# The cast of the second batch's first piece goes from GpSimd to ScalarE, in four parts, and four steps of a hand-set schedule change their visits

## The chip, the cores and the metric

The kernel runs on one core of one Trainium2 chip. The metric is the device time of one execution, in microseconds (us), lower is better. Every time below is of that one core. TensorE is called PE, VectorE DVE, ScalarE ACT, GpSimd POOL, and SyncE, which only issues DMAs here, SP.

## The reference

Per batch, 32 inducing vectors attend to the 12480 rows of `x` (giving `h`), then every row of `x` attends to the 32 rows of `h`; the result goes through a two-layer block with a PReLU-like step.

```python
B, N, m, C = (4, 12480, 32, 128)
n_tokens, d_model, d_ff = (49920, 128, 2048)

def mab(q, kv):
    s = scale * (q @ kv.transpose(0, 2, 1))
    s = s - s.max(-1, keepdims=True)
    a = np.exp(s)
    a /= a.sum(-1, keepdims=True) + 1e-09
    return a @ kv
h = mab(I, x)
x = mab(x, h).reshape(B * N, C)
h = x @ w_in
g = np.maximum(h, 0.0) + alpha * np.minimum(h, 0.0)
out = g @ w_out
```

## The kernel before, in words

**Tiles.** A batch's 12480 rows are cut into "supers" `s` of 2048 rows (16 tiles of 128), and a short rest of 192 rows. The first attention of a batch works on *pieces*, which are these supers in the order 0, rest, 1, 2, 3, 4, 5. `whole_pieces[p]` has index `p`, so the second batch's first piece is p=0 (super 0), its second is the short rest, the third p=2 (super 1), the fourth p=3 (super 2).

**First attention, per piece.** `a_load` brings the rows in as f32 (`xs`, 1024 KB, four buffers), `a_cast` makes them bf16 (`xn`, one POOL instruction of 128x2048, line 330), `a_turn` turns them by a DMA transpose on SP's queue (`xT`, line 353), `a_scores` and `a_least` give scores and their extreme, `a_exp` the exponentials `e1T` (ACT), `a_e1` turns those by a DMA transpose on SP's queue (line 446), `a_h`/`a_add` sum up. `a_cast_part` is a variant of the cast for a part of a piece, on an engine of choice; the start of the program uses it for the first batch (lines 347 and 349).

**Second attention, per super ("second rows").** Eight steps: `b_scores` (PE, line 641, and a copy from PSUM by ACT or DVE), `b_max` (DVE, line 718), `b_less_pool` (POOL, line 723), `b_exp` (ACT, line 685), `b_sum` (POOL: five additions of line 709 and `den`, line 733), `b_rec` (DVE, `rc`, line 746), `b_mul` (POOL, writes the attention weights four times over, `rep`, line 754), `b_turn` (a DMA transpose on SP's queue, `a<-rep`, line 763). Its result `a2` is what the second stage below multiplies.

**Blocks and visits.** The main loop goes over *visits*. A block is four tiles (512 rows) of one super; it has four visits, and a super 16. In a visit PE makes four products `hh` of 32x512 (`visit`, line 805, needs `a2` of its super), ACT and DVE turn each into a `gt` by ReLU (lines 818 and 820), and then PE makes the 16 products of the visit before (`second`, line 831). The linear part (line 858) is added by pairs of blocks. A finished block is copied out of PSUM (`finish`, lines 877, 884, 886) and stored by a DMA on SP's queue (line 891). The first super of the first batch is scaled only there, by the reciprocal `rec3` (`first_rec`, line 1164), whose sums POOL makes in `first_sum` (lines 709, 1151).

**What sets the order.** All work other than the main loop's is hung on visits by number with `at(n, fn, ..., cost=...)` and is issued after visit n's products, in the order in which it was registered: first the second-rows steps of all supers, then the pieces by p. Engines run their instructions in that order. SP's queue is in order as well: a DMA whose data isn't ready holds those behind it. `Plan.choose` searches, from hand-given costs of each step, which ReLU goes to ACT ("a") and which to DVE ("v"), which PSUM bank each product takes, and whether a step issued through `plan.then` runs in its visit or waits ("l") until the third ReLU of the next visit. It doesn't count POOL, nor DMAs.

For the first batch's super s=1 the visits of the eight steps are written by hand (`when`), and it is needed from visit 16 on; super 2 of the first batch is needed from visit 32 on. For the second batch's pieces p=0 to 3 the visits of load, cast and turn are written by hand too; p=0 is loaded ahead of the main loop. Scores of p=0 are at visit 19, of p=2 at 22, of p=3 at 30.

```python
            when = [1, 2, 3, 4, 5, 8, 8, 9]
```

```python
                load, cast, turn = {
                    0: (-1, 4, 6), 1: (-1, 9, 10), 2: (4, 10, 12), 3: (7, 16, 17)
                }.get(p, (load, cast, turn))
```

Of the kernel before, what the change touches and what calls it, by code (L numbers as in the profile page):

```python
# [24 lines left out]
BT = 4  # L25
# [5 lines left out]
def kernel(  # L31
# [239 lines left out]
    plan = Plan()  # L271
# [14 lines left out]
    def new_state(b):  # L286
        st = State()
        st.b = b
        st.pieces = whole_pieces if b else first_pieces
        st.np = len(st.pieces)  # L290
        st.xT = xt_pool.tile([C, NT, P], bf16, name="xT", tag="xT")
        st.xn, st.xs, st.s1, st.e1T, st.e1, st.s1p, st.hp = {}, {}, {}, {}, {}, {}, {}
        st.e2, st.m2, st.den2, st.rc, st.rep = {}, {}, {}, {}, {}

        st.mx = sm_pool.tile([P, NX], f32, name="mx", tag="mx")
        st.rm = sm_pool.tile([P, NX], f32, name="rm", tag="rm")
        st.fac = sm_pool.tile([P, NX], f32, name="fac", tag="fac")
        st.da = sm_pool.tile([P, NX], f32, name="da", tag="da")
        st.ex = sm_pool.tile([P, NX], f32, name="ex", tag="ex")
        st.den = sm_pool.tile([P, 1], f32, name="den", tag="den")  # L300
        st.hs = h_pool.tile([P, C], f32, name="hs", tag="hs")
        eng = nc.gpsimd if b else nc.vector
        eng.memset(st.mx[:], HIGH)
        eng.memset(st.da[:], 0.0)
        return st
# [18 lines left out]
    def a_cast(st, pc):  # L324
        s = pc.s
        r0, nt, last = supers[s]
        xs = st.xs[s]
        if pc.full:
            st.xn[s] = xn_pool.tile([P, ST, C], bf16, name="xn", tag="xn")
            nc.gpsimd.tensor_copy(out=st.xn[s][:], in_=xs[:])  # L330
        else:
            st.xn[s] = xn_left
            for t in range(nt):
                n = last if t == nt - 1 else P
                nc.gpsimd.tensor_copy(out=xn_left[:n, t, :], in_=xs[:n, t, :])

    def a_cast_part(st, pc, t0, n, eng):
        s = pc.s
        if not pc.full:
            a_cast(st, pc)  # L340
            return
        if s not in st.xn:
            st.xn[s] = xn_pool.tile([P, ST, C], bf16, name="xn", tag="xn")
        ts = slice(pc.t0 + t0, pc.t0 + t0 + n)
        to, of = st.xn[s][:, ts], st.xs[s][:, ts]
        if eng == "a":
            nc.scalar.copy(out=to, in_=of)
        else:
            (nc.gpsimd if eng == "p" else nc.vector).tensor_copy(out=to, in_=of)

    def a_turn(st, pc):
        s, nt = pc.s, pc.n
        nc.sync.dma_start_transpose(
            out=st.xT[:, tile0[s] : tile0[s] + nt, :],
            in_=st.xn[s][:, :nt, :].rearrange("p j c -> p (j c)"),
        )
# [326 lines left out]
    def b_exp(e, n):  # L683
        def work():
            nc.scalar.activation(out=e[:, :n], in_=e[:, :n], func=EXP, scale=scale)  # L685

        plan.then(work)
# [219 lines left out]
    st = new_state(0)  # L907
# [127 lines left out]
    def begin(step):  # L1035
# [39 lines left out]
        if f in "tc":  # L1075
            t0, n = cuts[pc.n][int(part)]
            if f == "t":
                kept["t", p, part] = a_turn_pe(st, pc, t0, n)
            else:
                a_turn_copy(st, pc, t0, n, kept.pop(("t", p, part)), act)  # L1080
        elif f == "k":
            a_cast_part(st, pc, *cuts[pc.n][int(part)], step[-1])
            done = first_pieces[int(p)].s
            if pc.full and step == last_cast[done]:
                load_next(done)
            if step == weights_after:
                load_weights()
        elif f == "u":
            kept["u", p] = a_e1_pe(st, pc)
        elif f == "v":  # L1090
            a_e1_copy(st, pc, kept.pop(("u", p)), act)
        else:
            {"s": a_scores, "m": a_least, "e": a_exp, "f": a_fac, "h": a_h, "g": a_add}[f](st, pc)
# [100 lines left out]
    def at(n, fn, *args, cost=()):  # L1194


        todo.setdefault(max(n, 0), []).append((fn, args, cost))
# [15 lines left out]
    for b, s, nt in groups[1:]:  # L1213
        n = first[b, s]
        when = [n - 23, n - 19, n - 16, n - 14, n - 13, n - 11, n - 9, n - 6]
        if (b, s) == (0, 1):
            when = [1, 2, 3, 4, 5, 8, 8, 9]
        if (b, s) == (0, 2):
            when[7] = n - 7
        at(when[0], on, b, b_scores, s, nt, cost=[("s", 25 * nt), ("f", 0)])  # L1220
        at(when[1], on, b, b_max, s, nt, cost=[("v", 70 + 33 * nt)])
        at(when[2], on, b, b_less_pool, s, nt)
        at(
            when[3],
            lambda b=b, s=s, nt=nt: b_exp(states[b].e2[s], nt),
            cost=[("a", 100 + 27 * nt)],
        )
        at(when[4], on, b, b_sum, s, nt)
        at(when[5], on, b, b_rec, s, nt, cost=[("v", 160)])
        at(when[6], on, b, b_mul, s, nt)  # L1230
        at(when[7], on, b, b_turn, s, 0, nt)
# [6 lines left out]
    def small_at(n, fn, *args, cost):  # L1238


        (kind, ns), *rest = cost
        at(n, fn, *args, cost=[(kind, ns + (0 if n in shared else TURNED)), *rest])
        shared.add(n)

    for b in range(B - 1):
        n = first[b, 0] - 1
        if b:
            at(n - 4, lambda b=b: states.__setitem__(b + 1, new_state(b + 1)))
        for p, pc in enumerate(whole_pieces):
            m = n + (8 * (p - 1) if p > 1 else p)  # L1250
            load, cast, turn = m - 3, m + 6, m + 8
            score = m + 15 if p > 1 else n + 16
            look = score + 1 + (p == 1)
            join = m + (24 if p == whole_pieces[-1].k else 23) if p > 1 else n + (31 if p else 23)
            if not b:
                load, cast, turn = {
                    0: (-1, 4, 6), 1: (-1, 9, 10), 2: (4, 10, 12), 3: (7, 16, 17)
                }.get(p, (load, cast, turn))
                score, look = (score, look) if p > 1 else (score + 4, look + 4)
                join = n + 31 if p < 2 else n + 39 if p < 4 else join  # L1260
            f = pc.full
            if load >= 0:
                at(load, on, b + 1, a_load, pc)
            at(cast, on, b + 1, a_cast, pc)
            at(turn, on, b + 1, a_turn, pc)
            small_at(
                score,
                on,
                b + 1,
                a_scores_least,  # L1270
                pc,
                cost=[("s", 215 if f else 85), ("v", 800 if f else 460)],
            )
            at(look, on, b + 1, a_exp, pc, cost=[("a", 717 if f else 430)])
            at(look + 2, on, b + 1, a_fac, pc, cost=[("a", 220)] if p else [])
            at(look + 1, on, b + 1, a_e1, pc)
            small_at(
                join, on, b + 1, a_h_add, pc, cost=[("s", 226 if f else 115), ("v", 260)]
            )
        m = n + 8 * (NS - 2) + 15  # L1280
        at(m + 2, on, b + 1, a_max, cost=[("a", 200)])
        at(m + 4, on, b + 1, a_factors, cost=[("s", 400), ("v", 70), ("a", 205)])
        at(m + 6, on, b + 1, a_parts, cost=[("a", 220), ("v", 260)])
        at(m + 8, on, b + 1, a_den, cost=[("s", 200), ("v", 370)])
        at(m + 12, on, b + 1, a_sum, cost=[("s", 200), ("v", 110)])
        small_at(m + 14, on, b + 1, a_w_both, cost=[("s", 220), ("a", 487)])
        small_at(m + 14, on, b + 1, a_lin, cost=[("s", 75), ("v", 190)])
# [4 lines left out]
    for n, (blk, i) in enumerate(visits):  # L1292
# [9 lines left out]
        cost = nt * Plan.FREE if both else 0  # L1302
# [55 lines left out]
```

## Time and profile before

| | |
|---|---|
| three runs | 597.59, 598.14, 598.18 us; median 598.14 us |
| the profiled execution | 596.33 us |
| its span in the trace | 594.5 us (1.83 us lie around it) |
| PE busy | 585.3 us, 98% of the span |
| DVE, ACT busy | 533.6 us (90%), 537.1 us (90%) |
| POOL busy | 218.6 us (37%) |
| granted TensorE clock | 1.0 |

Times in the trace count from the span's start. The main loop's first products stand at 30.0 us; a visit without extra products of PE takes 1.33 us. The table below gives, for finding one's way in the trace, where the `hh` products of a visit start.

| visit | 4 | 5 | 6 | 7 | 8 | 9 | 10 | 12 | 15 | 16 |
|---|---|---|---|---|---|---|---|---|---|---|
| us | 35.85 | 37.18 | 38.51 | 40.73 | 42.22 | 44.02 | 46.59 | 49.36 | 53.55 | 54.88 |

A group of instructions on one line of a timeline starts at the first column, lasts as long as the second, and may have in brackets the idle time of its engine before it and what ended it.

### The profile page before, as it was taken

What the parts mean: (1) busy time and instruction counts of PE and PEld (TensorE: products, weight loads), DVE (VectorE), ACT (ScalarE), POOL (GpSimd) and SP (SyncE); (2) the same over time, 40 slices, a digit from 0 to 9 for tenths busy, and PEclk for the clock granted to TensorE, in tenths of its full rate; (3) what the DMA queues carried; (4) which work ended last, traced back from release to release, by engine and by line L of the source; (5) the groups of instructions that cost most, each with busy time, mean ns of one, the idle gap of its engine ahead of it and who ended that gap; (6) DMA issues with size and microseconds to landing.
All of it is one profiled execution on the core that took longest, in us unless ns stands there. A gap on an engine that the chain in (4) does not pass through costs nothing.

```text
span 594.5 us, 23142 instructions
## 1 busy us (share of the span) xinstructions
PE 585.3 (98%) x9500; PEld 441.6 (74%) x9500; DVE 533.6 (90%) x975; ACT 537.1 (90%) x1085; POOL 218.6 (37%) x261
## 2 busy tenths in 40 slices
PE   9998999999999999999999999999999999999997
PEld 6676777777777777777777777777777777777776
DVE  5877999998999899998999989999999999989996
ACT  5787999999899999999999999999999998989986
POOL 3496525313416436323236156134134134144010
PEclk9999999999999999999999999999999999999999
DMA  8959799233177999541367999831321341433421
GB/s 340 272 176 222 186 233 176 70 100 83 45 205 159 242 205 198 126 82 55 78 162 171 192 238 195 170 92 46 91 72 55 92 75 53 118 76 65 91 69 47
DMA packets 122347, 80.56 MB, mean 136 GB/s; under 512 B 103760, under 2 KB 106112, under 8 KB 119168
## 3 DMA queue, kind: packets, MB, share of 16 engines
q1 hardware_dynamic: 122016, 78.99, 56.1%
q8 instruction: 74, 1.21, 0.9%
q14 instruction: 33, 0.27, 0.2%
q10 hardware_dynamic: 224, 0.09, 0.1%
HBM read 28.07 MB, written 25.56 MB: 90 GB/s over the span
## 4 chain that ended last, share of the span: by engine, by line
PE 89%; DMA 1%; POOL 1%; issue 0%; DVE 0%; DVEq 0%; ACT 0%
PE bp L831 63%; PE hh L805 21%; PE bp L858 2%; PE hh L641 1%; DMA a<-rep 1%; PE hh L470 1%; PE hh L376 1%; POOL rep L754 1%; DVE gt L820 0%; DVEq L1353 0%; PE hh L595 0%; PE hh L518 0%; PE hh L579 0%; PE hh L564 0%; PE hh L515 0%
## 5 line engine op out<-in xcount | busy, mean ns | idle before, releaser
L818 ACT ACTIVATE gt<-hh 128x512 bf16<-128x512 f32 x857 | 456.2, 604 | 38.4 <-PE hh L805 33.2
L820 DVE TENSOR_SCALAR gt<-hh 128x512 bf16<-128x512 f32 x703 | 451.4, 683 | 26.2 <-PE hh L805 14.8
L831 PE MATMUL bp<-W,gt 128*128 128x128 bf16 x6240 | 417.4, 220 | 0.3 <-DVE gt L820 0.2
L831 PEld LDWEIGHTS <-gt 128*128 128x128 bf16 x6240 | 349.3, 98 | 85.4 <-issue 76.6
L805 PE MATMUL hh<-a,HW 32*128 32x512 bf16 (+2 forms) x1664 | 156.0, 370 | 2.1 <-DMA a<-rep 1.6
L754 POOL TENSOR_TENSOR rep<-e,rc 128x2048 bf16<-128x2048 f32 (+1 forms) x24 | 84.5, 3521 | 25.7 <-DVE rc L746 25.3
L723 POOL TENSOR_TENSOR e<-e,smx 128x512 f32<-128x512 f32 (+1 forms) x24 | 24.6, 1027 | 158.1 <-ACT gt L818 81.3
L805 PEld LDWEIGHTS <-HW 32*128 32x128 bf16 x1664 | 40.6, 91 | 43.2 <-issue 7.2
L709 POOL TENSOR_TENSOR t<-e 128x256 f32<-128x256 f32 (+1 forms) x24 | 17.2, 718 | 139.8 <-ACT e L685 139.8
L884 ACT COPY ob<-bp 128x512 f32<-128x512 f32 (+1 forms) x62 | 36.3, 585 | 4.3 <-PE bp L831 1.4
L330 POOL CAST xn<-xs 128x2048 bf16<-128x2048 f32 x18 | 34.0, 1891 | 0.5
L709 POOL TENSOR_TENSOR t<-t 128x128 f32<-128x128 f32 (+3 forms) x100 | 30.5, 305 | 7.8
L886 DVE COPY ob<-bp 128x512 f32<-128x512 f32 x32 | 21.9, 685 | 6.1 <-PE bp L831 6.1
L858 PEld LDWEIGHTS <-a 32*128 32x128 bf16 x392 | 15.0, 93 | 6.0 <-issue 0.3
L390 DVE TENSOR_SCALAR_CACHE_REDUCE s<-hh 128x512 f32<-128x512 f32 (+2 forms) x29 | 17.9, 618 | 1.6 <-PE hh L376 1.6
L858 PE MATMUL bp<-HA,a 32*128 32x128 bf16 x392 | 19.1, 214 | 0.0
L415 ACT ACTIVATE e1T<-s,rm 128x512 bf16<-128x512 f32 (+1 forms) x25 | 17.9, 718 | 0.7 <-DVE rm L399 0.7
L718 DVE TENSOR_REDUCE smx<-e 128x16 f32<-128x512 f32 (+1 forms) x24 | 15.9, 661 | 0.0
L960 PE MATMUL bp<-blank 128*128 128x256 bf16 x78 | 14.4, 322 | 1.2 <-DVE blank L906 1.2
L685 ACT ACTIVATE e<-e 128x512 f32<-128x512 f32 (+1 forms) x24 | 15.0, 624 | 0.0
L699 ACT COPY e<-hh 128x512 f32<-128x512 f32 (+1 forms) x23 | 13.9, 604 | 0.7 <-PE hh L641 0.6
L486 DVE SCALAR_TENSOR_TENSOR hs<-hs,fac,hh 128x128 f32<-128x128 f32 (+1 forms) x25 | 8.6, 344 | 6.5 <-PE hh L470 5.5
(110 smaller groups left out, 201.5 us busy)
## 6 DMA issues: line engine op xcount, KB each, us to landing
out_dram<-ob SPq DMA_DIRECT2D x97, 256.0 KB, 2.6
xs<-in_x_dram SPq DMA_DIRECT2D x23, 1024.0 KB, 6.3
xs<-in_x_dram SPq DMA_DIRECT2D x2, 512.0 KB, 9.0
w_in_f<-in_moe_w_in_dram SPq DMA_DIRECT2D x1, 1024.0 KB, 4.8
a<-rep SPq DMA_TRANSPOSE x25, 5.2
xT<-xn SPq DMA_TRANSPOSE x18, 5.4
e<-e1T SPq DMA_TRANSPOSE x18, 2.7
xs_left<-in_x_dram SPq DMA_DIRECT2D x4, 64.0 KB, 5.0
```

What stands on the lines that cost most here:

```text
L330: nc.gpsimd.tensor_copy(out=st.xn[s][:], in_=xs[:])
L390: nc.vector.tensor_scalar(out=s1[:parts, :cols], in0=ps[:parts, :cols], scalar1=-scale, scalar2=None, op0=MULT, op1=MIN, accum_out=st.mx[: ...
L709: nc.gpsimd.tensor_tensor(out=t[:, :n], in0=src[:, :n, :w], in1=src[:, :n, w : 2 * w], op=ADD)
L723: nc.gpsimd.tensor_tensor(out=st.e2[s][:, :n], in0=st.e2[s][:, :n], in1=st.m2[s][:, :n].unsqueeze(2).broadcast_to([P, n, M]), op=SUB,)
L754: nc.gpsimd.tensor_tensor(out=rep[:, :n], in0=st.e2[s][:, :n].unsqueeze(2).broadcast_to([P, n, R, M]), in1=rc[:, :n].unsqueeze(2).unsqueez ...
L805: nc.tensor.matmul(hh[:, q * cols + w.start : q * cols + w.stop], HWs[b][rows, v * P : (v + 1) * P], a2[rows, t0 : t0 + nt, :].rearrange(" ...
L818: nc.scalar.activation(out=gt[:, :cols], in_=hh[:, :cols], func=RELU)
L820: nc.vector.tensor_relu(gt[:, :cols], hh[:, :cols])
L831: nc.tensor.matmul(blk.acc[:, t * C : (t + 1) * C], gt[:, (q * nt + t) * P : (q * nt + t + 1) * P], W1[:, k, :], start=(not blk.begun), st ...
L858: nc.tensor.matmul(blk.acc[w, t * C : (t + 1) * C], blk.a2[rows, blk.t0 + t, w], HAs[b][rows, :], start=(not blk.begun and t == 0), stop=F ...
L884: nc.scalar.copy(out=ob[:, :nt], in_=acc)
L886: nc.vector.tensor_copy(out=ob[:, :nt], in_=acc)
```

## The change

- The cast of the second batch's p=0 leaves POOL (visit 4, one instruction of 128x2048). It becomes four ACT copies of 128x512, issued through `plan.then` in visits 4, 5, 5 and 6, each with a cost of 560 ns of ACT in the plan; its DMA transpose goes from visit 6 to 7.
- For the second rows of super 1 of the first batch, `b_rec` goes from visit 8 to 7 and `b_turn` from 9 to 8. `b_mul` stays at 8.
- p=2 is cast at visit 9 instead of 10 and turned at 11 instead of 12.
- p=3 is loaded at visit 12 instead of 7, cast at 20 instead of 16 and turned at 21 instead of 17.

```diff
+    def a_cast_act(st, pc, t0, n):
+        plan.then(lambda: a_cast_part(st, pc, t0, n, "a"))
...
         if (b, s) == (0, 1):
-            when = [1, 2, 3, 4, 5, 8, 8, 9]
+            when = [1, 2, 3, 4, 5, 7, 8, 8]
...
                 load, cast, turn = {
-                    0: (-1, 4, 6), 1: (-1, 9, 10), 2: (4, 10, 12), 3: (7, 16, 17)
+                    0: (-1, -1, 7), 1: (-1, 9, 10), 2: (4, 9, 11), 3: (12, 20, 21)
                 }.get(p, (load, cast, turn))
...
-            at(cast, on, b + 1, a_cast, pc)
+            if cast >= 0:
+                at(cast, on, b + 1, a_cast, pc)
+            else:
+                for q, v in enumerate((4, 5, 5, 6)):
+                    at(v, on, b + 1, a_cast_act, pc, q * BT, BT, cost=[("a", 560)])
```

## The prediction

> **What bounds the kernel now.** The page comes first, for the engine shares and the chain of work that ended last.
>
> ```profile
> PE 585.3 (98%) x9500; PEld 441.6 (74%) x9500; DVE 533.6 (90%) x975; ACT 537.1 (90%) x1085; POOL 218.6 (37%) x261
> ...
> PE 89%; DMA 1%; POOL 1%; issue 0%; DVE 0%; DVEq 0%; ACT 0%
> ```
>
> PE is busy for 98% of the span and carries 89% of the chain. The change removes no PE work, so it can win only what PE waits. Where it waits is in the table of waits, asked for the stretch of the edited visits, 37 to 57 us:
>
> ```profile
> DVE rc L746 <- POOL den L733: 1.8, 1, 1.8
> PE hh L805 <- DMA a<-rep: 1.6, 1, 1.6
> ...
> PE hh L641 <- DVE ob L877: 0.7, 1, 0.7
> ```
>
> PE waits twice here, and the timeline of PE places both waits:
>
> ```profile
> 42.69 0.40 PE L858 MATMUL bp<-HA,a 32*128 32x128 bf16 x8
> ...
> 46.11 0.55 PE L641 MATMUL hh<-hT,xT 128*128 128x32 bf16 x16 [0.70 <-DVE ob L877]
> ...
> 56.57 0.40 PE L805 MATMUL hh<-a,HW 32*128 32x512 bf16 x4 [1.62 <-DMA a<-rep]
> ```
>
> One is 0.70 us at visit 9, for the PSUM bank that DVE's first `ob` copy frees; the other 1.62 us at visit 16, for the turned second rows of super 1. Together 2.32 us, the most that this place can give. Their common cause stands in the timelines of POOL and DVE.
>
> ```profile
> 40.80 1.89 POOL L330 CAST xn<-xs 128x2048 bf16<-128x2048 f32 x1
> 42.66 0.73 POOL L709 TENSOR_TENSOR t<-e 128x256 f32<-128x256 f32 x1
> ...
> 45.02 0.20 POOL L733 TENSOR_SCALAR den<-t 128x16 f32<-128x16 f32 x1
> 45.65 3.61 POOL L754 TENSOR_TENSOR rep<-e,rc 128x2048 bf16<-128x2048 f32 x1 [0.42 <-issue]
> ```
>
> ```profile
> 42.34 0.29 DVE L618 CAST HA<-hh 128x128 bf16<-128x128 f32 x1 [0.40 <-PE hh L616]
> 42.75 0.69 DVE L820 TENSOR_SCALAR gt<-hh 128x512 bf16<-128x512 f32 x1
> 45.26 0.25 DVE L746 RECIPROCAL rc<-den 128x16 f32<-128x16 f32 x1 [1.82 <-POOL den L733]
> 45.43 1.22 DVE L877 TENSOR_TENSOR ob<-bp,rec 128x512 f32<-128x512 f32 x2
> ```
>
> POOL makes the cast of the second batch's p=0 ahead of the sums of the second rows. So `den` is late; DVE, in order, stands 1.82 us before the reciprocal with the `ob` copies behind it (first wait); and `rep` starts at 45.65, after which SP's queue and the landing of its transpose decide:
>
> ```profile
> 42.72 1.92 SPq L353 DMA_TRANSPOSE xT<-xn  x1
> 44.68 1.28 SPq L315 DMA_DIRECT2D xs<-in_x_dram  x1
> 46.09 0.94 SPq L891 DMA_DIRECT2D out_dram<-ob  x2
> 49.29 3.60 SPq L763 DMA_TRANSPOSE a<-rep  x1
> ```
>
> ```profile
> 49.29 7.24 DMA a<-rep
> ```
>
> The second row is from the chain in order of time: issue to landing took 7.24 us, up to 56.53.
>
> **The change part by part.** *The cast leaves POOL.* Its slot is 42.66 - 40.80 = 1.86 us. The sums take 45.22 - 42.66 = 2.56 us, so `den` is there at 40.80 + 2.56 = 43.36 instead of 45.22.
>
> *`b_rec` one visit earlier.* It now follows `HA` of visit 7, which ends at 42.63. DVE waits 43.36 - 42.63 = 0.73 us instead of 1.82; behind the waiting instruction are one ReLU of visit 8 (0.69 us) and the `ob` copies. Reciprocal 43.40 to 43.65, ReLU to 44.3, first `ob` copy (half of 1.22) to about 44.9; its block is closed on PE by 43.09. PE wants the bank at 46.11 - 0.70 = 45.41. The first wait goes, with 0.5 us to spare.
>
> *`rep` and its turn.* `rep` followed the start of the reciprocal by 45.65 - 45.26 = 0.39 us and the turn followed `rep`'s start by 3.64, so it is issued at 43.40 + 4.03 = 47.43 instead of 49.29. All turns of this kind landed as in this row of the view of the tile `a`, and the one next after, whose row in the DMA view follows, in 4.4 us:
>
> ```profile
> DMA to landing us min/median/max: 2.7/5.2/7.2
> ```
>
> ```profile
> a<-rep SPq DMA_TRANSPOSE x1, 4.4
> ```
>
> It lands at 50.1 to 54.6, by the median at 52.6. Visit 16 would want it at 56.57 - 1.62 - 0.70 = 54.25. I take the median, as the 1024 KB load that preceded it at 44.68 moves to visit 12, behind it: no wait, 1.6 us to spare. At 7.2 us, 0.4 us of wait stay. Issuing the turn in visit 8 instead of 9 costs nothing, as no DMA stands between.
>
> [...]
>
> *Four casts on ACT.* Their price is between back-to-back work on ACT (4.04 / 8 = 0.505 us) and the same cast at the program's start (0.62 us):
>
> ```profile
> 49.84 4.04 ACT L818 ACTIVATE gt<-hh 128x512 bf16<-128x512 f32 x8 [0.24 <-PE hh L805]
> ```
>
> ```profile
> L347 ACT CAST xn<-xs x5: 602/619/1058, 6.2 to 17.9; 128x512 bf16<-128x512 f32 x3, 128x1024 bf16<-128x1024 f32 x2
> ```
>
> So 2.0 to 2.5 us more for ACT in visits 4 to 7. What hides them is idle time of ACT and DVE, by stretches (columns: length, then PE, PEld, DVE, ACT, POOL busy):
>
> ```profile
> 37.00:41.25 4.25, 4.25 (x69) 3.26 (x67) 3.01 (x8) 3.67 (x9) 3.79 (x9) 1.00 0.59 123
> 41.25:46.10 4.85, 4.16 (x68) 3.16 (x66) 2.51 (x6) 4.60 (x9) 4.03 (x8) 1.00 1.00 219
> ```
>
> Idle in the first: ACT 4.25 - 3.67 = 0.58, DVE 4.25 - 3.01 = 1.24, together 1.82. In the second: 0.25 and 2.34, together 2.59, of which 1.82 was the blocked reciprocal. The plan knows the casts' price and can move ReLUs to DVE. What doesn't fit into the first stretch is 0.2 to 0.7 us, on two engines 0.1 to 0.35 us of delay; PSUM banks leave little slack, so I take 0.3 us of PE. Bounds: no gain, since work is only added; at worst all four fall on PE's path, 2.5 us.
>
> [...]
>
> ```profile
> L349 DVE CAST xn<-xs x2: 427/556/686, 6.2 to 6.5; 128x512 bf16<-128x512 f32 x1, 128x1024 bf16<-128x1024 f32 x1
> ```
>
> On DVE the four would be 4 x 0.427 = 1.7 us, which fits into the 1.82 idle; by it the sum would be 0.3 us better than what I give the change.
>
> *p=2 one visit earlier* costs nothing: its cast still comes after `rep` on POOL, its turn after the second rows' turn on SP.
>
> *p=3 later.* Its cast comes to POOL at visit 20, ahead of `rep` of super 2, which ran from 66.91 and ended at 70.52, while SP took it only at 73.16: 2.6 us of slack for a cast of 1.89.
>
> ```profile
> 66.91 3.61 POOL L754 TENSOR_TENSOR rep<-e,rc 128x2048 bf16<-128x2048 f32 x1 [1.62 <-DVE rc L746]
> ```
>
> Its turn goes into SP's queue at visit 21, behind the first row here and ahead of the others; the last is super 2's turn:
>
> ```profile
> 66.13 1.19 SPq L446 DMA_TRANSPOSE e<-e1T  x1
> 67.42 1.81 SPq L446 DMA_TRANSPOSE e<-e1T_left  x1
> 70.81 1.64 SPq L446 DMA_TRANSPOSE e<-e1T  x1
> 72.54 0.53 SPq L891 DMA_DIRECT2D out_dram<-ob  x1
> 73.16 2.42 SPq L763 DMA_TRANSPOSE a<-rep  x1
> ```
>
> ```profile
> L353 SPq DMA_TRANSPOSE xT<-xn x18: 1339/3227/6987, 42.7 to 376.9; - x18
> ```
>
> ```profile
> 80.20 0.61 PE L805 MATMUL hh<-a,HW 32*128 32x512 bf16 x4
> ```
>
> All in the old kernel's clock, since this stage moves forward as a whole: 67.32 + d + 1.81 + 1.64 + 0.53 = 71.30 + d is when super 2's turn is issued, d being the issue time of p=3's turn (1.3 to 7.0, median 3.2); with landing L it must be there by 80.20. No wait while d + L is under 8.9 us. Medians: 3.2 + 5.2 = 8.4. I take no wait.
>
> *The plan.* `choose` runs anew, and every ReLU after visit 4 may change engines. Bounds from what PE's weight loads wait for ReLUs from 57 us to the end:
>
> ```profile
> PEld L831 <- DVE gt L820: 1.3, 6, 0.4
> ...
> PEld L831 <- ACT gt L818: 0.5, 2, 0.2
> ```
>
> Between -1.8 (all gone) and +1.8 (doubled); I take 0, the costs after visit 9 being the same.
>
> Sum: -1.62 - 0.70 + 0.3 = -2.0 us. The profiled execution's 596.33 becomes 594.3; the runs' median, 1.81 above it, 598.14 becomes 596.1. About 0.2% (1.2 us) is what a measurement can tell from no change: faster is below 596.9, slower above 599.3.
>
> **The rivals.** *The casts are not covered.* ACT runs them in order, the ReLUs of visits 5 to 7 come late, and PSUM banks don't come free. For it: 1.82 us of idle time in visits 5 and 6 against 2.0 to 2.5 of work. Against it: the product of the linear weights after visit 6 gives PE 1.06 us of other work, in which ACT and DVE can catch up, and DVE gains 1.1 us.
>
> ```profile
> 39.74 1.06 PE L993 MATMUL hh<-AW,winT 128*128 128x128 bf16 x16
> ```
>
> At four back-to-back casts, 2.0 us, the sum is -2.32 + 2.0 = -0.3: 597.8, no change.
>
> *SP's queue takes the place of POOL (slower).* Place: super 2's turn before visit 32. It decides from d + L = 8.9; at 10.9 the gain is gone, and from 12.1 the kernel is slower by over 0.2%. With d = 5.9 and L = 7.2, 13.1, the wait is 4.2 us: 596.1 + 4.2 = 600.3. For it: the median sum is only 0.5 us short of the first bound. Against: its own load has long left the queue by then, and the 7.24 above stood right behind a load.
>
> *The change doesn't do what it says.* ACT's last part ends two us after the 42.72 at which the `xT` turn is issued now, the turn holds SP, and the second rows land as slowly as before: 47.43 + 7.24 = 54.67, 0.4 us too late. The gain is then 1.6 us, 596.5; still faster.
>
> *The new plan is worse*, by the 1.8 us above: 597.9.
>
> **How the numbers follow.** The forecast with its neighbour of 596.5: 0.62. Casts uncovered: 0.15. Queue: 0.13. A worse plan: 0.07. The rest, 0.03, for a better plan, faster. Of the queue's share 0.03 stops at no change, and of the worse plan's 0.04 does (its bound is no change, and 0.03 is for more than it). Faster 0.62 + 0.03 = 0.65, same 0.15 + 0.03 + 0.04 = 0.22, slower 0.10 + 0.03 = 0.13. The forecast's own range is 595.0 to 596.9. For 8 in 10 the upper end takes in the uncovered casts, the worse plan and the smaller queue waits, 599.0; the lower end takes the casts as free (0.3) and half of the plan's bound, 595.0.
>
> **What would show it.** Right: no wait of `hh` for `a<-rep` at visit 16; `den` at 43.4; DVE's wait before the reciprocal under 1 us; `rep` from about 43.8; the `L641` product of visit 9 unhindered; four ACT copies of 0.5 to 0.6 us between 38 and 43 us; fewer ReLUs on ACT there. Wrong: PE pieces stretched between 38 and 43 us by more than 0.5 us (casts); a wait for `a<-rep` at visit 32 (queue); or the loss spread after 90 us (plan).

## The result, and the profile after

| | before | changed |
|---|---|---|
| median of 6 runs | 598.12 us | 593.68 us |
| lowest, highest | 597.59, 598.42 us | 593.25, 594.53 us |
| profiled execution, its span | 596.33, 594.5 us | 593.70, 591.9 us |

The ratio is 0.9928 with a 95% interval of 0.9915 to 0.9941: 0.7% faster, 4.4 us. The forecast was 2.0 us, with a range that ended at 595.0. The two profiled executions are 2.6 us apart; the other 1.8 us lie between the profiled execution of before and its runs.

The page after, PE's row, and from the waits between 37 and 57 us the two that answer to those of before (line numbers are higher by 3):

```profile
PE 584.5 (99%) x9500; PEld 441.3 (75%) x9500; DVE 535.5 (90%) x978; ACT 537.3 (91%) x1086; POOL 216.6 (37%) x260
```

```profile
DVE rc L749 <- POOL den L736: 0.9, 1, 0.9
...
PE bp L861 <- DVE HA L621: 0.2, 1, 0.2
```

Both waits of PE that the prediction showed are gone: no row `hh<-a` for the second rows, none of `L641` for an `ob` copy. In their place stands a short one, for `HA`. The timeline of PE:

```profile
42.24 0.77 PE L808 MATMUL hh<-a,HW 32*128 32x512 bf16 x4
43.24 0.40 PE L861 MATMUL bp<-HA,a 32*128 32x128 bf16 x8 [0.22 <-DVE HA L621]
...
44.57 0.70 PE L808 MATMUL hh<-a,HW 32*128 32x512 bf16 x4
...
46.10 0.56 PE L644 MATMUL hh<-hT,xT 128*128 128x32 bf16 x16
46.59 0.39 PE L808 MATMUL hh<-a,HW 32*128 32x512 bf16 x4
...
54.77 0.39 PE L808 MATMUL hh<-a,HW 32*128 32x512 bf16 x4
```

`L644` follows without a wait, but it starts at 46.10, as before, since the products of visits 8 and 9 took 0.77 and 0.70 us (0.49 and 0.39 before) and PE waited for `HA`, the weights of the linear part, which DVE copies out of PSUM: the first 0.70 us were won and lost again. Visit 16 starts at 54.77 instead of 56.57. POOL, DVE, ACT and SP, in that order:

```profile
43.81 0.20 POOL L736 TENSOR_SCALAR den<-t 128x16 f32<-128x16 f32 x1
44.44 3.61 POOL L757 TENSOR_TENSOR rep<-e,rc 128x2048 bf16<-128x2048 f32 x1 [0.42 <-issue]
```

```profile
41.40 0.25 DVE L1167 RECIPROCAL rec<-den 128x16 f32<-128x16 f32 x1 [0.49 <-POOL den L1154]
...
41.72 1.27 DVE L823 TENSOR_SCALAR gt<-hh 128x512 bf16<-128x512 f32 x2
42.91 0.28 DVE L621 CAST HA<-hh 128x128 bf16<-128x128 f32 x1
44.05 0.25 DVE L749 RECIPROCAL rc<-den 128x16 f32<-128x16 f32 x1 [0.86 <-POOL den L736]
44.22 0.63 DVE L823 TENSOR_SCALAR gt<-hh 128x512 bf16<-128x512 f32 x1
44.76 1.27 DVE L880 TENSOR_TENSOR ob<-bp,rec 128x512 f32<-128x512 f32 x2
```

```profile
39.48 0.60 ACT L347 CAST xn<-xs 128x512 bf16<-128x512 f32 x1
...
40.48 1.13 ACT L347 CAST xn<-xs 128x512 bf16<-128x512 f32 x2
...
42.47 0.63 ACT L347 CAST xn<-xs 128x512 bf16<-128x512 f32 x1
```

```profile
43.12 1.93 SPq L356 DMA_TRANSPOSE xT<-xn  x1
48.07 1.78 SPq L766 DMA_TRANSPOSE a<-rep  x1
49.95 1.56 SPq L894 DMA_DIRECT2D out_dram<-ob  x2
```

```profile
a<-rep SPq DMA_TRANSPOSE x1, 4.3
```

The second rows land 4.3 us after their issue, at 52.4, 2.4 us before PE wants them. Note the queue: not only the fourth piece's load has gone from ahead of this turn; the two output stores, too, now stand behind it.

Visit by visit, the changed kernel's lead over the kernel before in the two traces is 0.0 us at visit 10, 1.80 at 16, 2.16 at 34, about 2.2 from there to 300, 2.4 at 340 and 2.6 at the end.

### The profile page after: what moved, and what is told of

Read it like the earlier page. It is cut to its first block, busy times and chain, and to the rows that moved or that the text cites. A ratio compares the mean times of both kernels' runs of the same rounds, so it can differ in the third digit from the quotient of the medians.

```text
span 591.9 us, 23144 instructions
## 1 busy us (share of the span) xinstructions
PE 584.5 (99%) x9500; PEld 441.3 (75%) x9500; DVE 535.5 (90%) x978; ACT 537.3 (91%) x1086; POOL 216.6 (37%) x260
## 4 chain that ended last, share of the span: by engine, by line
PE 91%; DMA 5%; POOL 2%; DVE 0%; issue 0%; DVEq 0%; SPq 0%; ACT 0%; POOLq 0%
PE bp L834 64%; PE hh L808 21%; DMA xs<-in_x_dram 3%; PE bp L861 2%; DMA w_out_f<-in_moe_w_out_dram 2%; PE hh L644 2%; PE hh L473 1%; PE hh L379 1%; DMA e<-e1T 1%; POOL W L977 1%; POOL AW L986 1%; POOL t L712 0%; DVE gt L823 0%; DVEq L1360 0%; DVE xn L349 0%
## 5 line engine op out<-in xcount | busy, mean ns | idle before, releaser
L330 POOL CAST xn<-xs 128x2048 bf16<-128x2048 f32 x17 | 32.1, 1888 | 2.8 <-DMA xs<-in_x_dram 2.3
```

## The experiments

Four theories. *POOL*: the cast ahead of the sums is why the second rows are late. *Queue*: what stands ahead of their turn in SP's queue is why. *ACT and plan*: the casts on ACT cost 0.7 us, or the new choices of engines bring the gain. *Length of the wait*: the kernel before loses more, in most of its executions, than its first trace shows.

### The kernel before, four more times

> The kernel before, unchanged, once more with a trace. Two theories of the 1.8 us by which the forecast fell short of the runs. Representative trace: the wait for the second rows at visit 16 is again 1.6 us and the span near 594.5, and then the missing 1.8 us lie elsewhere. Unrepresentative trace: the profiled execution of before was a lucky one; this one has a span near 596.3 and a wait at visit 16 of 2.5 to 3.5 us, with POOL starting its chain of weights later than 28.4 us.

> The kernel before, unchanged, one more trace. The runs go from 595.4 to 600.2 us, the traces seen are of 596.3 and 597.2. If the queue theory holds, the time outside the wait at visit 16 is the same in every trace (594.7 us plus or minus 0.6), and the wait alone makes the difference: 1.6 us at 596.3, 2.5 at 597.2, and here the device time less 594.7.

> The kernel before, unchanged, another trace, for the spread of its runs. Queue theory: device time less 594.7 us is the wait at visit 16, as in the three traces so far (1.6 at 596.3, 2.3 at 597.1, 2.5 at 597.2). Else the extra time shows at another place.

> The same once more, since single executions differ by up to 5 us: device time less 594.7 us is the wait at visit 16, or else the extra time shows at another place.

The twelve runs of the first lay between 595.41 and 600.20 us (median 599.25; ratio to the others of the same kernel 1.0007, 0.9988 to 1.0027). Five traces of one kernel, the first being that of the prediction:

| device time, us | loop starts at | wait at visit 9 | wait at visit 16 | loss at visits 16 to 19, with a lower clock |
|---|---|---|---|---|
| 596.33 | 30.00 | 0.70 | 1.62 | - |
| 597.09 | 29.93 | 1.01 | 2.29 | - |
| 597.20 | 30.01 | 0.87 | 2.49 | - |
| 597.32 | 32.27 | - | 1.43 | - |
| 599.54 | 30.57 | 1.24 | 2.24 | 1.5 |

The trace that the prediction was made from is the fastest of the five. "Device time less 594.7 is the wait" fits the second and third and fails for the last two: one began its loop 2.3 us later and got part of that back, and the last has something new. From the start of visit 16 to the end, the device time of the first four is 539.6 to 539.8 us and that of the last 541.2: the spread lies ahead of visit 16, in the start of the loop and in the two waits, and in that something new. After its wait, the 16 products of a visit take up to 1.89 us, against 1.07 at a clock of 1.00:

```profile
58.30 0.40 PE L805 MATMUL hh<-a,HW 32*128 32x512 bf16 x4 [2.24 <-DMA a<-rep]
58.63 1.33 PE L831 MATMUL bp<-W,gt 128*128 128x128 bf16 x16
59.89 0.61 PE L805 MATMUL hh<-a,HW 32*128 32x512 bf16 x4
60.44 1.89 PE L831 MATMUL bp<-W,gt 128*128 128x128 bf16 x16
```

The stretches of the same execution (the column after the five engines is the granted clock):

```profile
60.00:61.00 1.00, 1.00 (x10) 0.57 (x7) 1.00 (x3) 0.41 (x1) 0.00 (x0) 0.50 1.14 267
61.00:62.00 1.00, 1.00 (x12) 1.00 (x10) 0.33 (x1) 1.00 (x3) 0.00 (x0) 0.50 0.82 305
```

The clock stood at 0.64 to 0.50 from 59 to 62 us, though the wait of 2.49 us in another execution was followed by a clock of 1.00 throughout (to 66 us). So the length of the wait alone does not decide it: waits of 2.24 us here and 2.06 us in e11 were followed by a clock of 0.50, the longer one was not. What does decide it is not shown.

### The load alone, later or sooner

```diff
# e2, in the kernel before
-3: (7, 16, 17)
+3: (12, 20, 21)
# e8, in the kernel before
-3: (7, 16, 17)
+3: (5, 16, 17)
```

> The kernel before with only the fourth piece moved (load, cast and turn at visits 12, 20, 21 instead of 7, 16, 17). The plan's costs and so all choices of engines are those of before. If the load ahead in the queue makes the second rows late: their landing falls from 7.2 to about 4.4 us and the time falls by 1.6 to 2.8 us. If the cast on POOL is the cause: the landing gets a little shorter at most, 0 to 1 us. If the later turn of the fourth piece delays super 2: slower by up to 1 us.

> The kernel before with one edit: the fourth piece's load at visit 5 instead of 7, so it stands in SP's queue ahead of the first piece's turn instead of behind it. POOL's order and the plan are those of before. Queue theory (the turn, waiting for POOL's cast, holds the load until 44.7 us, the load is still moving when the second rows' turn is issued at 49.3, and how long it lasts differs from run to run): landing of the second rows 4.4 to 6 us instead of 7.2 to 8.1, time down by 2.5 to 3 us as with the load later, spread of the runs about 2 us instead of 5. POOL theory (the second rows are late because POOL makes them late, the load is a bystander): within 1 us of the kernel before, same spread.

e2: 594.72 us, ratio 0.9951 (0.9934 to 0.9968). e8: 594.84, ratio 0.9959 (0.9943 to 0.9975); its runs span 1.9 us, e2's the same. In both, POOL casts ahead of the sums as before. With the load at visit 5 it leaves at 38.3, ahead of the turn of the first piece:

```profile
38.26 1.07 SPq L315 DMA_DIRECT2D xs<-in_x_dram  x2
42.40 4.78 SPq L353 DMA_TRANSPOSE xT<-xn  x1
47.28 1.00 SPq L891 DMA_DIRECT2D out_dram<-ob  x2
48.98 1.35 SPq L763 DMA_TRANSPOSE a<-rep  x1
```

The second rows land 4.3 us after issue in e8 and 6.1 in e2 (with 0.48 us of wait left at visit 16). By the ratios, one number in the table of visits (e8) gives 0.41% and three (e2) 0.49% of the change's 0.72%: the queue theory holds, and the load was no bystander. What is left is the wait at visit 9 (0.9 and 0.8 us), which POOL's order causes.

### The cast alone, behind the second rows on POOL

```diff
-0: (-1, 4, 6)
+0: (-1, 9, 10)
```

> The kernel before with only the first piece's cast moved on POOL, from visit 4 (ahead of the second rows' sums) to visit 9 (behind their product), its turn to visit 10. ACT gets nothing, the plan is that of before. If POOL's order is the cause, the sums come 1.9 us sooner, both waits of PE go (0.70 and 1.62 us in the trace) and the time falls by 2 us or more, as much as the whole change or more since ACT's price is saved: 593 to 596 us. If the new plan is the cause of the gain, under 1 us.

593.43 us, ratio 0.9934 (0.9916 to 0.9952): within the intervals the whole gain of the change, with nothing on ACT and the choices of engines of before. DVE finds the sums ready, and PE the bank:

```profile
43.35 0.25 DVE L746 RECIPROCAL rc<-den 128x16 f32<-128x16 f32 x1
```

```profile
45.07 0.56 PE L641 MATMUL hh<-hT,xT 128*128 128x32 bf16 x16
```

It isn't a test of POOL alone, though: with the first piece's turn gone from visit 6, nothing holds the load, which left at 38.5; in the first trace of before it left at 44.68, behind that turn, issued at 42.72.

### The load put back into the changed kernel, with the reciprocal early or late

```diff
# e4, in the changed kernel
-3: (12, 20, 21)
+3: (7, 16, 17)
# e10, in the changed kernel
-when = [1, 2, 3, 4, 5, 7, 8, 8]
+when = [1, 2, 3, 4, 5, 8, 8, 9]
# e11: both
```

> The changed kernel with the fourth piece put back (load, cast, turn at visits 7, 16, 17); the plan is that of the changed kernel. If the load matters: the second rows land in about 7 us instead of 4.3, at 55 instead of 52.4 us, and 0.3 to 1 us of wait come back at visit 16. If POOL's order alone matters: within 0.5 us of the changed kernel.

> The changed kernel with the second rows' reciprocal and turn put back (visits 8, 8, 9 instead of 7, 8, 8). The only difference in DVE's order: the reciprocal stands behind the ReLU of visit 8 instead of ahead of it. If the early reciprocal is what costs PE 0.7 us in visits 8 to 10 (DVE waits 0.86 us before it with a ReLU and the output copies behind): that wait falls to 0.3 us or less, the products of visits 8 and 9 are no longer stretched, 0.5 to 0.9 us faster, near 593.0. If the four ACT casts are what costs: the same time as the changed kernel within 0.2 us.

> As the one before, and the fourth piece put back too (load, cast and turn at visits 7, 16, 17). With both put back it should keep the gain at visit 10 and not have the tight place before visit 32, where the changed kernel's super 2 landed about when PE wanted it: near 593, and runs above 594 become rare. If the load ahead of the turn still hurts: 0.3 to 1 us of wait at visit 16, near 593.7.

e4: 593.75 us, 0.9930 (0.9910 to 0.9949). e10: 593.72, 0.9944 (0.9924 to 0.9963). e11: 598.48, 1.0018 (1.0001 to 1.0036): no gain at all, against my expectation of 593 to 593.7. POOL is relieved in all three. What differs is the order in SP's queue. e11 and then e4:

```profile
45.02 0.98 SPq L315 DMA_DIRECT2D xs<-in_x_dram  x1
46.10 1.25 SPq L894 DMA_DIRECT2D out_dram<-ob  x2
47.91 4.87 SPq L766 DMA_TRANSPOSE a<-rep  x1
```

```profile
45.70 1.37 SPq L315 DMA_DIRECT2D xs<-in_x_dram  x1
48.72 3.12 SPq L766 DMA_TRANSPOSE a<-rep  x1
51.94 1.00 SPq L894 DMA_DIRECT2D out_dram<-ob  x2
```

From issue to landing in us, again e11 and then e4:

```profile
a<-rep SPq DMA_TRANSPOSE x1, 8.5
```

```profile
a<-rep SPq DMA_TRANSPOSE x1, 5.2
```

| issued in the 5 us ahead of the turn, besides the first piece's turn | landing, us | kernels |
|---|---|---|
| load, then two stores | 7.2 to 8.5 | before (all five traces), e11 |
| load | 5.2 | e4 |
| two stores | 4.3 to 6.1 | e8, e2, e10, e3 |
| nothing | 4.3 | changed kernel |

In e11 the turn is issued at 47.91, 1.4 us sooner than in the first trace of before, and still lands at 56.4, 8.5 us later. So POOL's order alone is not enough, and the POOL theory, which was mine, falls as the main cause of the wait at visit 16: the load and the stores together, just ahead of the turn, make the second rows late. Whether the turn then stands in the queue behind them or shares the DMA engines with them, these runs don't separate. Turning in visit 8 instead of 9 takes the stores from ahead of it, and the load's move takes the load; either is enough. e11's wait of 2.06 us was again followed by a clock of 0.50 (57 to 60 us).

e10 bears on the loss up to visit 10. The only difference in DVE's order is that the reciprocal stands behind the ReLU of visit 8:

```profile
43.36 0.69 DVE L823 TENSOR_SCALAR gt<-hh 128x512 bf16<-128x512 f32 x1
44.17 0.25 DVE L749 RECIPROCAL rc<-den 128x16 f32<-128x16 f32 x1
```

No wait there, and from the start of the loop to visit 10 it is 0.76 us quicker than the first trace of the changed kernel. But only 0.31 us of this come behind the reciprocal. From visit 9 to visit 10 PE needs 2.02 us where the reciprocal is early (e4, e7 and that trace; 1.90 in e16, the second trace of the changed kernel) and 1.71 us where it is late (e10, e11). The other 0.46 us are lost at visit 8, and `HA`, for which PE waits there, stands ahead of the second rows' reciprocal in DVE's order. `HA` was late because DVE had waited 0.49 us for POOL's sums of the first super (the reciprocal of line 1167), with two ReLUs between it and `HA`. In e10, whose loop began 0.58 us later, and in e16 there is no such wait; their rows of this reciprocal:

```profile
41.53 0.25 DVE L1167 RECIPROCAL rec<-den 128x16 f32<-128x16 f32 x1
```

```profile
41.04 0.25 DVE L1167 RECIPROCAL rec<-den 128x16 f32<-128x16 f32 x1
```

From the start of its loop to visit 10 the changed kernel needed 16.56 us in the first trace and 15.99 in e16, against 15.80 in e10. The kernel before waits 0.98 us for the same sums and loses nothing by it: its choices of engines have one ReLU there, not two.

e10 lost 1.0 us again at visit 48, where super 3's second rows were late behind two turns that took 7.20 and 6.23 us to issue (6.51 and 4.88 in the changed kernel):

```profile
76.62 7.20 SPq L356 DMA_TRANSPOSE xT<-xn  x1
...
87.93 6.23 SPq L356 DMA_TRANSPOSE xT<-xn  x1
```

```profile
103.24 0.40 PE L808 MATMUL hh<-a,HW 32*128 32x512 bf16 x4 [1.01 <-DMA a<-rep]
```

### The changed kernel with nothing on ACT

```diff
-plan.then(lambda: a_cast_part(st, pc, t0, n, "a"))
+plan.then(lambda: None)
...
+            if cast < 0:
+                turn = 10
+                at(9, on, b + 1, a_cast, pc)
             at(turn, on, b + 1, a_turn, pc)
```

> The changed kernel with the four ACT casts left out of ACT, while the plan still counts them (so all choices of engines are those of the changed kernel); the cast is done by POOL at visit 9, behind the second rows' product, its turn at visit 10. If the four casts cost PE 0.7 us in visits 7 to 10, as the stretched products of the changed kernel suggest: 0.7 us faster than the changed kernel, near 593.0. If that loss comes from the plan's choices and DVE's waits: within 0.2 us.

598.89 us, 1.0019 (1.0005 to 1.0034), slower by 5 us than the changed kernel, for a reason that neither theory had. Up to visit 10 the answer is clear: while ACT idles, PE stands within 0.2 us of the changed kernel's first trace, with a wait of 0.33 us for `HA` and the same 0.70 us for the products of visit 9. The four casts cost PE at most 0.2 us; the rest of the loss has the two causes found with e10. Then, at visit 32:

```profile
65.61 1.89 POOL L330 CAST xn<-xs 128x2048 bf16<-128x2048 f32 x1 [2.16 <-DMA xs<-in_x_dram]
```

```profile
75.90 2.93 SPq L766 DMA_TRANSPOSE a<-rep  x1
```

```profile
82.43 0.61 PE L808 MATMUL hh<-a,HW 32*128 32x512 bf16 x4 [4.01 <-DMA a<-rep]
```

The first piece's turn at visit 10 pushed the fourth piece's load back, POOL waited for it, its turn took 4.12 us to issue and super 2's second rows landed 4 us late; the clock stood at 0.50 from 82 to 88 us, 2.2 us more. That is the prediction's rival of SP's queue before visit 32, in a kernel one step away. How near the changed kernel is to it, its own queue shows; super 2's turn landed in 5.4 us, at 78.3, and visit 32 began at 78.39 (in e16 78.1 and 78.16):

```profile
66.28 3.00 SPq L356 DMA_TRANSPOSE xT<-xn  x1
69.38 1.19 SPq L449 DMA_TRANSPOSE e<-e1T_left  x1
...
72.93 2.31 SPq L766 DMA_TRANSPOSE a<-rep  x1
```

### 1.04 us more on POOL in the changed kernel

```diff
-            for i in range(NV):
+            for i in (*range(NV), NV - 1):
                 linear_weights(i)
```

> The changed kernel with 1.04 us more on POOL ahead of the second rows (the last quarter of the linear weights is made twice). The second rows landed 2.4 us before PE needed them, so at visit 16 nothing should be lost; through the reciprocal that DVE waits for, up to 1.04 us could be lost at visits 8 to 10. Slack theory: under 0.3 us in all. If POOL's sums still set PE's time: 1 us slower.

595.04 us, 0.9962 (0.9944 to 0.9979), 1.4 us slower than the changed kernel: the slack theory fails. In the trace there is indeed no wait at visit 16, but 0.5 us more are lost by visit 9, where DVE's wait for the first super's sums has grown from 0.49 to 0.99 us, and 0.73 at visit 48, at a place where I had counted no slack.

### PE kept busy in the wait

```diff
+        if blk.k == ST // BT and i == 0:
+            for _ in range(14):
+                nc.tensor.matmul(hhs[0][:, : 2 * P], blank[:, :P], blank[:], start=True, stop=True)
         segments = [(st.b, slice(0, cols))]
```

> The kernel before with 14 products of no use (128x256, into a PSUM bank that visit 16 overwrites) put on PE ahead of visit 16, where it waits for the second rows; at 0.11 us each they fill 1.5 us of the wait. Nothing else differs. In the look at a slow execution of before, and in two other runs with a wait of 2 to 4 us, the granted clock stood at 0.5 for some 3 us after the wait and the next products took 1.3 to 1.5 us longer. If this clock loss is what makes the runs of before slower than its first trace: the median falls by 0.5 to 1.5 us though PE has more to do, runs above 599 us become rare, and the granted clock is 1.0 in the trace. If the spread comes from the wait's length alone: no change, 597.4 to 597.8, spread as before.

597.53 us, 0.9997 (0.9980 to 1.0014), runs of 596.76 to 599.12. Its trace has a clock of 1.00 and the rest of the wait:

```profile
55.87 1.69 PE L795 MATMUL hh<-blank 128*128 128x256 bf16 x14
58.23 0.40 PE L808 MATMUL hh<-a,HW 32*128 32x512 bf16 x4 [0.68 <-DMA a<-rep]
```

The median moved by 0.7 us, inside the interval. How often the kernel before pays the clock loss is not settled by this; that it does so in some executions the traces show.

### What is good without what gives back

```diff
# e15 and e18: e7's edit, and in the changed kernel
-when = [1, 2, 3, 4, 5, 7, 8, 8]
+when = [1, 2, 3, 4, 5, 8, 8, 9]
-2: (4, 9, 11), 3: (12, 20, 21)
+2: (4, 10, 12), 3: (7, 16, 17)
# e16: the changed kernel; e17: e3
```

> The choices of engines of the changed kernel, but the reciprocal and the turn of the second rows put back (8, 8, 9), no cast on ACT, the first piece's cast on POOL at visit 9 with its turn at 10, third and fourth piece as before (4, 10, 12 and 7, 16, 17). It joins what the runs showed to be good: no wait at visits 8 to 10, the load out of the way of the second rows' turn, the queue free before visits 32 and 48. If these are the causes: 592.5 to 593.2, below both kernels, spread under 2 us. If not: a wait for second rows at visit 16, 32 or 48 and 593.5 or more.

> The changed kernel once more, on the same chip as the next two. Its runs were 593.25 to 594.53 us. If the place before visits 32 and 48 is tight in it, as its trace says (second rows of super 2 landed when PE wanted them), some runs lose up to 1 us there and the trace shows a wait for second rows at one of the two.

> The kernel before with only the first piece's cast moved on POOL behind the second rows, once more beside the changed kernel. If the change's whole gain is that POOL and SP's queue get out of the way of the second rows, and ACT's part adds nothing: the same time as the changed kernel or up to 0.7 us faster (no wait at visits 8 to 10). If ACT's casts or the new plan add a gain of their own: 0.5 us or more slower than the changed kernel.

> The version with the changed kernel's choices of engines and none of the give-backs found, once more beside the changed kernel. In its trace it gained 0.76 us on the changed kernel at visits 9 and 10 and kept it, while its main loop began 0.79 us later. If that later start was chance: 0.5 to 0.8 us faster than the changed kernel. If not: the same time.

e15: 593.49 us, 0.9931 (0.9905 to 0.9957), above the 592.5 to 593.2 expected. Then together on one chip: the changed kernel 593.75, 0.9932 (0.9917 to 0.9948); e17 594.29, 0.9942 (0.9928 to 0.9955); e18 593.37, 0.9934 (0.9918 to 0.9951). In its traces the e15/e18 kernel has no wait for second rows anywhere and is 0.7 us quicker than the first trace of the changed kernel between the start of the loop and visit 10, and keeps 0.6 of it. Against e16 it is only 0.1 to 0.2 us quicker there, and nothing is left at the end; loops start between 29.6 and 30.8 us from execution to execution, and the intervals overlap. No version was shown to beat the changed kernel. e17 starts ahead by the same 0.7 us of the first trace and loses it after visit 200, where its choices of engines are those of before. The kernels of e17 and e18 differ in these choices alone, and so do those of e3 and e15: from visit 16 to the end the new choices are 1.0 and 0.7 us quicker in the traces, but the intervals of the runs overlap.

## Why the prediction was right or wrong

**Right.** Both waits and their places, and the chain from cast to `den` to `rep` as far as it sets when the turn is issued: 48.07 instead of 49.29 us. The wait at visit 16 went whole, by way of a landing of 4.3 us, better than the 5.2 taken. `den` came 1.2 us sooner, not 1.86: the cast is gone in full, but POOL's sums of the first super, ahead of it, start at 38.9 instead of 38.2 us in the two traces, since POOL's weights came 0.6 us later. The casts on ACT took 0.5 to 0.6 us each, and moving them was hidden but for at most 0.2 us of PE (e7). In the traces the forecast of 2.0 us stands against 1.80 us at visit 16 and 2.6 at the end.

**Wrong, and it made most of the miss: "the runs' median, 1.81 above it".** I carried the difference between the profiled execution and the runs over to the changed kernel as if it were a constant. In three of the four further traces of before it was time in the very waits that the change removes, and what followed from them. Of five executions of before the one profiled first was the fastest; the waits of three others were up to 0.9 us longer at visit 16 and 0.5 at visit 9, and one lost 1.5 us to the clock. Of the changed kernel, the profiled execution (593.70) is its median (593.68). Visit 16 began at 56.57 to 58.30 us in the five traces of before and at 54.77 and 54.40 in the two of the changed kernel; from there to the end the device time is 539.6 to 539.8 us (541.2 with the lower clock) against 538.9 and 538.8. The means of the five and the two are 4.0 us apart, the runs 4.4. What share each of these has in the 1.8 us is not settled.

**Wrong: "Their common cause stands in the timelines of POOL and DVE."** For the wait at visit 9 the cast is the cause: it stays in e2 and e8, where the cast stays, and goes in e3. For the wait at visit 16 it isn't: in e11 the cast is gone, the turn is issued 1.4 us sooner, and PE waits 2.06 us. The load and the stores ahead in SP's queue decide there. The sum took the load's move into account, but only as the choice of the median landing.

**Wrong: "Issuing the turn in visit 8 instead of 9 costs nothing, as no DMA stands between."** The two output stores stand between: ahead of the turn in the kernel before, behind it in the changed one. The change had a part with a gain of its own that I costed at nothing. e4 against e11 prices it: 593.75 against 598.48 with the load ahead. Beside the load's move it adds nothing that the runs show (e10, 593.72).

**Wrong: the reciprocal at visit 7.** I let DVE wait 0.73 us (measured 0.86) and took the ReLU behind it as free. It cost PE 0.3 us at visit 9 in the first trace (0.2 in e16). Another 0.5 us at visit 8 had no term in the sum at all: `HA`, late behind DVE's wait for the first super's sums and the ReLU that the new choices had added. In that trace the two took back the 0.70 us of the first wait; in e16 the second was gone.

**Wrong size: the casts on ACT,** 0.3 us taken, at most 0.2 measured in e7. The 1.82 us into which four casts on DVE were said to fit are the idle time of ACT and DVE together; DVE alone had 1.24.

**Plan.** Taken as 0 with bounds of 1.8: the lead grew by 0.4 us at visits 32 to 34 and by 0.4 after 300. The traces of e17 and e18 make the new choices a likely cause; their runs don't show it.

**The rivals.** Uncovered casts: no. The late `xT` turn: it was issued at 43.12 instead of 42.72 and held nothing up. A worse plan: no. The queue before visit 32: not in the changed kernel, whose super 2 landed with nothing to spare, but it came true in e7 (4.01 us) and one super later in e6 and e10.

## What to carry to other kernels

The wait for the second rows' transfer at visit 16 took 1.43 to 2.49 us in five executions of the kernel before. So when a change removes such a wait, count the excess of the runs over the profiled execution as part of it, and take several executions before fixing the size. For a transfer that is late, write down what stands ahead of it in its queue: here the load and two stores together cost 3 to 4 us (landings of 7.2 to 8.5 us against 4.3) and either alone 0 to 2 (4.3 to 6.1), and moving one number in a table gave over half of the gain. A step that waits should stand behind the work that its engine could do meanwhile, not ahead of it: here the reciprocal ahead of a ReLU cost PE 0.3 us at visit 9 in one trace and 0.2 in another.

## What was not expected of the hardware

A wait of PE of 2.06 to 2.24 us was followed in two executions by a granted clock of 0.50 for about 3 us, which cost 1.5 us more, and in another execution a wait of 2.49 us was not. The same DMA transpose took 4.3 to 8.5 us to land, by what was issued in the 5 us before it.
